# A transformer block on one core: token loads moved ahead of the weights, and side projections as whole-array matmuls

## The chip, the core and the metric

The kernel runs on one core of a Trainium2 chip. The core has a matrix engine (TensorE, PE in the profile, with its weight loads shown apart as PEld), a vector engine (VectorE, DVE), a scalar engine (ScalarE, ACT), a general engine (GpSimd, POOL) and a queue for transfers (SyncE, SP). The metric is the device time of one execution in microseconds.

## The reference

One block with two parallel branches on the same normalized input, 2048 tokens of width 512, 32 heads of 16:

```python
x = A_x                                   # [1, 2048, 512] bf16
xn = (x - mean) / sqrt(var + 1e-5)        # over the last axis
q, k, v = split(xn @ wqkv)                # 32 heads, 16 wide
p = softmax(q @ k.T / 4)                  # 2048 x 2048 for each head
attn = (p @ v) @ wo
h = silu(xn @ w1) * (xn @ w3)             # 512 -> 1792
return x + attn + h @ w2
```

## The kernel before

**The order is written by a planner.** A Python loop in `_build` keeps a clock for each engine, asks each engine's picker (`pick_pe`, `pick_act`, `pick_dve`, `pick_pool`, `pick_sp`) for its next candidate, emits the earliest, and notes what it reads and writes. The result is a fixed instruction stream for each engine, with semaphore waits between them. So a constant such as `TOL` or `A_LEAD` changes nothing in an instruction, but it changes where instructions stand.

**Attention.** The work is cut into units of one group of four heads and 256 queries (128 at the start and the end). It is done in two passes over the scores.

- Pass 1 (`p1_cand`, matmuls at L1011): score pairs, [128 queries x 512 keys] for two heads side by side, written to PSUM banks 0 and 1 or 2 and 3 in turn. VectorE takes the maximum over the keys (TENSOR_REDUCE at L1051, 1024 columns at a time, 1018 of them; three more pairs go through a custom instruction at L1040). A pair's banks are free again once its maximum is taken, so at most two pairs stand ahead of VectorE.
- The negated maximum of each query is then put into two spare rows of the queries (`tile_QT2`, the tiles named AQ, near the start and the end; a transpose by DMA for the rest), so that pass 2 produces scores with the maximum already subtracted.
- Pass 2 (`p2_cand`, matmuls at L1273): scores transposed, [128 keys x queries], 512 columns to a block, 2048 blocks, in banks 4 to 7. ScalarE takes the exponential (L1286, one block; L1316, two blocks in one instruction where two neighbours are ready) and writes PT.
- PT times the values with a column of ones (`tile_PV`) gives numerator and denominator.

Score matmuls contract over 32 rows only, so they use a quarter of the array's rows each, and up to four run at once ("row" mode of the planner).

**Side tiles.** Everything else on TensorE is a side tile: projections to keys, queries and values, gate and up projections, the output product (`tile_OUT`, `tile_OUTA`, `tile_OUTB`), and filler matmuls (`fill_cand`, `warm_cand` at L1626) whose result nobody reads, which are emitted when little else ran lately. All but the transposes (L645) and the warm-up go through one helper, `col_groups` (L552): a group is four matmuls of [128 rows x 32 columns], one for each column quarter of the array, that stream the same 512 columns side by side. `pick_pe` places a group, or its half of 256 columns, ahead of a waiting score matmul when it ends before that one is due:

```python
if c[0] + c[2] <= late + TOL:
    return c[0], c[1]
...
if len(c) > 3:
    if c[0] + _c_mm(256) <= late + TOL:
        return c[0], c[3]
```

The planner charges 0.106 us for a change from column groups to score rows and 0.092 us for the change back (`pe_start`).

**The head.** `LOADS = (0, "k", "q", 4, 8, 12)`: four token tiles of 128 tokens, key weights, query weights, then the other tokens, and value weights behind them, 512 KB each, all issued on SP in this order. VectorE takes each tile's statistics (L583, L586), GpSimd the inverse deviation (L596, L599), VectorE (L612) or GpSimd (L622) normalizes, as `NORM` says for each group of two tiles; TensorE transposes (L645) and ScalarE copies the transposed tile out (L652). ScalarE also pads the key and query weights (L523, L525) and takes the statistics of tiles 8 to 15 (L573, L577). When four tiles are there, `tile_KT(0)` projects their 512 keys in four groups of 512 columns, and `tile_QT` their 512 queries; ScalarE copies both out (L668, L764), and pass 1 can begin.

**The tail.** After the last maximum come the last unit's AQ tile and its copy (L782), its exponentials, its value product, a reciprocal (L1371), a product (L1373), the last output group, and the store.

Of the kernel before, what the change touches and what calls it, by code (L numbers as in the profile page):

```python
# [36 lines left out]
class _Prog:  # L37
# [3 lines left out]
    def __init__(self):  # L41
        self.ops = {e: [] for e in _ENGS}
        self.reg = {}
        self.ndma = 0
        self.dma_last = [None] * _NDMA_SEMS
        self.dma_final = [0] * _NDMA_SEMS
        self.free = {e: 0.85 for e in _ENGS}
        self.rg = [0.0] * 4
        self.pe_mode = "col"
        self.pe_vis = 0.0  # L50
        self.act_end = 0.0
# [83 lines left out]
    def pe(self, fn, reads, writes, mode, groups, dur, name="", first=None):  # L135
# [8 lines left out]
        start = self.pe_start(mode, groups, ready)  # L144
        if start < _COLD:
# [101 lines left out]
def _build(nc, A_x, A_wqkv, A_wo, B_w1, B_w3, B_w2, out):  # L247
# [15 lines left out]
    TOL = 0.02  # L263
    PV_LEFT = 4
    ROW_LEAD = 0.45
    PAIR_WAIT = 0.0
# [32 lines left out]
    FFN_HI = 600  # L299
# [11 lines left out]
    RECENT_MIN = 9400.0  # L311
# [27 lines left out]
    with ctx:  # L339
# [133 lines left out]
        NORM = "ddddpppp"  # L473
# [72 lines left out]
        def col_groups(bk, make_lhsT, rhs_ap, ncols, c0=0, start=True, stop=True, m=32, skip=False, n=4):  # L546
            def part(a, b, start, skip):
                def f(e):
                    for i in range(n):
                        kw = dict(skip_group_check=True) if skip else {}  # L550
# [4 lines left out]
                    return ins  # L555
                return f
# [7 lines left out]
        def ln_chunk(gi):  # L564
# [16 lines left out]
            else:  # L581
# [3 lines left out]
                for t in tl:  # L585
                    dveq.append(_Item(lambda e, t=t: e.bn_aggr(mv[:, t, :], stats[:, t, :]), [("st", t)], [("mv", t)],  # L586
                                      0.075, 0.2, pred=lambda t=t: ("st", t) in done, cb=lambda op: mv_done(op)))
# [39 lines left out]
        def tr_ready(t):  # L627
# [3 lines left out]
            if t % XG == XG - 1:  # L631
                gi = t // XG
                head_tiles.append(tile_KT(gi))
                if gi == 0:
                    head_tiles.append(tile_QT())

        def tile_tr(t):
# [11 lines left out]
            def evac(bk):  # L649
# [6 lines left out]
                         pred=lambda: ("xn", t) in done and (t < 4 or "QTg" in done))  # L656


        def tile_KT(sc):
            groups = []  # L660
            for c in range(DC):
                groups.append((lambda bk, c=c: col_groups(
                    bk, lambda i: wpad["k", 0][:, c, 32 * i:32 * i + 32],
# [3 lines left out]
            def evac(bk):  # L667
# [4 lines left out]
            return _Tile("KT0_%d" % sc, groups, evac,  # L672
                         pred=lambda: "wk0" in done
                         and all(("xnT", t) in done for t in range(sc * 4, sc * 4 + 4)))
# [3 lines left out]
        def tile_heads(what, g0, ng, sc, need):  # L678
# [4 lines left out]
            def grp(c):  # L683
                return lambda bk: col_groups(bk, lambda i: w[:, c, 64 * g0 + 32 * i:64 * g0 + 32 * i + 32],
# [45 lines left out]
        def tile_V(t, need=None):  # L730
            groups = []
            for c in range(DC):
                groups.append((lambda bk, c=c: col_groups(
                    bk, lambda i: xnT[:, c, t * 128 + 32 * i:t * 128 + 32 * i + 32], lambda i: wv[:, c, :], D,
# [12 lines left out]
        def qt_groups(qc, g, q0, nq, stop_last):  # L747
            groups = []
            for c in range(DC):
                groups.append((lambda bk, c=c: col_groups(  # L750
                    bk, lambda i: wpad["q", g][:, c, 32 * i:32 * i + 32],
# [5 lines left out]
        def qt0_done(op):  # L757
            done.add(("QT", 0))
            miscq.extend(act_stats[PRE_STATS:])

        def tile_QT():
            def evac(bk):
                done.add("QTg")
                return [_Item(lambda e: e.activation(QT[:, 0, :], bank(bk), ACTF.Identity),  # L764
                              [("ps", bk)], qh_keys(0, 0, 512), _c_act(512),
                              cb=qt0_done)]
            return _Tile("QT0", qt_groups(0, 0, 0, 512, True), evac,
                         pred=lambda: "wq0" in done and all(("xnT", t) in done for t in range(4)))

        def tile_QT2(u):  # L770
# [4 lines left out]
            for qt in range(nq // 128):  # L775
                groups.append((lambda bk, qt=qt: col_groups(
                    bk, lambda i: Z[:, par, qt, 32 * i:32 * i + 32], lambda i: ident[:, :], 128, c0=qt * 128,
# [18 lines left out]
        def ffn_pair(sc, fc):  # L796
# [18 lines left out]
            def groups(which):  # L815
                return [(lambda bk, c=c: col_groups(
                    bk, lambda i: w13[:, sl, which * DC + c, 32 * i:32 * i + 32],
# [3 lines left out]
            def zg_done(op):  # L821
                lazyq.append(_Item(lambda e: e.activation(th[:, ss, :], zg[:, ss, :], ACTF.Tanh),  # L822
                                   [("zg", ss)], [("th", ss)], _c_act(512), cb=part_done))
# [1082 lines left out]
```

## Time and profile before

| | us |
|---|---|
| runs shown (3) | 1202.22, 1201.60, 1201.04; median 1201.60 |
| profiled execution, its own time | 1200.68 |
| its span, first to last instruction | 1199.0 |
| VectorE busy | 1174.9 |
| ScalarE busy | 1167.5 |
| TensorE busy | 1152.8 |
| GpSimd busy | 453.6 |
| granted TensorE clock, mean | 0.999 of full speed |

The profiled execution's span is what all timeline positions count from; its own time is 1.68 us longer, and the median of the runs shown is 0.92 us above that. Busy time is the sum of the records of an engine where they do not overlap; a record includes the time from its start to the landing of its last result, so that two records that follow each other closely overlap, and a mean duration is longer than the beat at which such instructions follow each other. A bracket behind a timeline row gives the idle time ahead of it and what ended that.

### The profile page before, as it was taken

What the parts mean: (1) busy time and instruction counts of PE and PEld (TensorE: products, weight loads), DVE (VectorE), ACT (ScalarE), POOL (GpSimd) and SP (SyncE); (2) the same over time, 40 slices, a digit from 0 to 9 for tenths busy, and PEclk for the clock granted to TensorE, in tenths of its full rate; (3) what the DMA queues carried; (4) which work ended last, traced back from release to release, by engine and by line L of the source; (5) the groups of instructions that cost most, each with busy time, mean ns of one, the idle gap of its engine ahead of it and who ended that gap; (6) DMA issues with size and microseconds to landing.
All of it is one profiled execution on the core that took longest, in us unless ns stands there. A gap on an engine that the chain in (4) does not pass through costs nothing.

```text
span 1199.0 us, 44560 instructions
## 1 busy us (share of the span) xinstructions
PE 1152.8 (96%) x19488; PEld 476.3 (40%) x19488; DVE 1174.9 (98%) x1069; ACT 1167.5 (97%) x2210; POOL 453.6 (38%) x908
## 2 busy tenths in 40 slices
PE   9999999999999999999999999999999999999997
PEld 4443333343334433333334333333333343345554
DVE  8999999999999999999999999999999999999994
ACT  7799999999999999999999999999999999999997
POOL 4345655642212257442222236652222126233320
PEclk9999999999999999999999999999999999999999
DMA  6423214230001132210001122210000111001000
GB/s 194 117 51 91 64 40 112 44 71 25 20 19 33 31 70 50 53 33 21 22 16 27 33 59 48 62 42 20 23 20 20 36 47 25 19 22 22 23 12 25
DMA packets 131231, 52.86 MB, mean 44 GB/s; under 512 B 100068, under 2 KB 131036, under 8 KB 131036
## 3 DMA queue, kind: packets, MB, share of 16 engines
q1 hardware_dynamic: 131036, 50.01, 16.8%
q8 instruction: 153, 2.51, 0.9%
q14 instruction: 42, 0.34, 0.1%
HBM read 38.73 MB, written 6.74 MB: 38 GB/s over the span
## 4 chain that ended last, share of the span: by engine, by line
PE 47%; ACT 42%; DVE 9%; issue 1%; DMA 1%; POOL 1%; SPq 0%
ACT PT L1286 28%; PE ps L552 26%; PE ps L1273 13%; ACT PT L1316 9%; DVE part L1051 8%; PE ps L1011 7%; ACT zg L828 1%; ACT th L822 1%; ACT U L1381 1%; ACT ub L832 1%; ACT kq L723 1%; PE ps L645 0%; DMA PT<-in_A_x_dram 0%; DMA R<-rd 0%; POOL hT L811 0%
## 5 line engine op out<-in xcount | busy, mean ns | idle before, releaser
L1051 DVE TENSOR_REDUCE part<-ps 128x2 f32<-128x1024 f32 x1018 | 1154.8, 1212 | 1.5 <-PE ps L1011 0.5
L1286 ACT ACTIVATE PT<-ps 128x512 bf16<-128x512 f32 x1630 | 864.7, 631 | 9.5 <-PE ps L1273 4.9
L1273 PE MATMUL ps<-QT,KT 32*128 32x256 bf16 (+1 forms) x4672 | 536.0, 259 | 6.2 <-ACT PT L1316 5.6
L1011 PE MATMUL ps<-KT,QT 32*128 32x512 bf16 x2042 | 421.3, 384 | 1.6 <-DVE part L1051 1.5
L1273 PEld LDWEIGHTS ps<-QT,KT 32*128 32x128 bf16 x4672 | 203.1, 92 | 225.7 <-issue 89.9
L1316 ACT ACTIVATE PT<-ps 128x1024 bf16<-128x1024 f32 x209 | 221.6, 1081 | 0.0
L552 PE MATMUL ps<-xnT,ident 128*32 128x512 bf16 (+1 forms) x2620 | 198.1, 353 | 19.0 <-ACT PT L1316 9.8
L1406 POOL TENSOR_TENSOR Rc<-Lc,mone 128x8 f32<-128x8 f32 (+1 forms) x70 | 105.9, 1513 | 224.1 <-DMA Lc<-U 224.0
L552 PE MATMUL ps<-PT,Vaug 128*17 128x256 bf16 (+1 forms) x4672 | 179.8, 261 | 3.2 <-ACT PT L1316 2.1
L552 PE MATMUL ps<-xnT,w 128*32 128x512 bf16 (+1 forms) x2204 | 153.1, 345 | 6.5 <-ACT PT L1316 2.5
L1011 PEld LDWEIGHTS ps<-KT,QT 32*128 32x128 bf16 x2042 | 106.5, 91 | 131.7 <-issue 67.3
L552 PEld LDWEIGHTS ps<-PT,Vaug 128*17 128x17 bf16 x4672 | 87.1, 90 | 82.7 <-issue 60.7
L552 PEld LDWEIGHTS ps<-xnT,ident 128*32 128x32 bf16 x2620 | 54.3, 94 | 105.5 <-ACT PT L1286 46.7
L1158 POOL TENSOR_TENSOR mx<-part 128x16 f32<-128x16 f32 (+1 forms) x67 | 14.1, 210 | 174.4 <-DVE part L1051 174.4
L552 PEld LDWEIGHTS ps<-xnT,w 128*32 128x32 bf16 x2204 | 44.0, 95 | 81.6 <-issue 44.5
L552 PE MATMUL ps<-w,hT 128*32 128x256 bf16 (+1 forms) x1160 | 76.0, 336 | 0.0
L1426 POOL TENSOR_TENSOR wk_on<-U,R 128x256 bf16<-128x256 f32 (+1 forms) x37 | 23.4, 632 | 128.9 <-DMA R<-rd 128.9
L811 POOL TENSOR_TENSOR hT<-a,t 128x512 bf16<-128x512 f32 x56 | 71.2, 1271 | 2.3
L809 POOL TENSOR_TENSOR a<-zg,ub 128x512 f32<-128x512 bf16 x56 | 64.6, 1153 | 7.9 <-ACT ub L832 7.4
L1426 POOL TENSOR_TENSOR on_b<-U,R 128x256 bf16<-128x256 f32 (+1 forms) x33 | 23.5, 711 | 96.8 <-DMA R<-rd 96.6
L807 POOL TENSOR_SCALAR t<-th 128x512 f32<-128x512 bf16 x56 | 34.6, 619 | 27.6 <-ACT th L822 26.6
L822 ACT ACTIVATE th<-zg 128x512 bf16<-128x512 bf16 x56 | 39.2, 700 | 0.0
(98 smaller groups left out, 543.3 us busy)
## 6 DMA issues: line engine op xcount, KB each, us to landing
w<-in_B_w_dram SPq DMA_DIRECT2D x112, 128.0 KB
R<-rd SPq DMA_DIRECT2D x55, 128.0 KB
QT<-qd SPq DMA_DIRECT2D x31, 128.0 KB
KT<-kd SPq DMA_DIRECT2D x28, 128.0 KB
PT<-in_A_x_dram SPq DMA_DIRECT2D x4, 512.0 KB
xr<-in_A_x_dram SPq DMA_DIRECT2D x16, 128.0 KB
out_dram<-osb SPq DMA_DIRECT2D x16, 128.0 KB
qd<-kq SPq DMA_DIRECT2D x15, 128.0 KB
```

The source lines that it names most:

```text
L552: ins = e.matmul(bank(bk)[32 * i:32 * i + m, c0 + a:c0 + b], make_lhsT(i), rhs if (a, b) == (0, ncols) else rhs[:, a:b], start=start, stop ...
L807: q.append(_Item(lambda e: e.tensor_scalar(t1[:, :], th[:, ss, :], 1.0, 1.0, ALU.mult, ALU.add), [("th", ss)], [("t1",)], 0.62, 0.72))
L809: q.append(_Item(lambda e: e.tensor_tensor(a32[:, :], zg[:, ss, :], ub[:, ss, :], ALU.mult), [("zg", ss), ("ub", ss)], [("a32",)], 1.1, 1.25))
L811: q.append(_Item(lambda e: e.tensor_tensor(hT[:, hslot(idx), :], a32[:, :], t1[:, :], ALU.mult), [("a32",), ("t1",)], [("hT", hslot(idx))] ...
L822: lazyq.append(_Item(lambda e: e.activation(th[:, ss, :], zg[:, ss, :], ACTF.Tanh), [("zg", ss)], [("th", ss)], _c_act(512), cb=part_done))
L1011: ins = e.matmul(bank(2 * sl + i), QT[32 * j:32 * j + 32, qs, q * 128:(q + 1) * 128], KT[32 * j:32 * j + 32, g, c_ * 512:(c_ + 1) * 512], ...
L1051: redq.append(_Item(lambda e: e.tensor_reduce(dst, pair_ap.rearrange("p (a b) -> p a b", b=512), AX.X, ALU.max), writes, [("part", par, qt ...
L1273: ins = e.matmul(bank(b)[:, i * nq:(i + 1) * nq], KT[32 * j:32 * j + 32, g, (k0 + i) * 128:(k0 + i + 1) * 128], QT[32 * j:32 * j + 32, qs, ...
L1286: expq.append(_Item(lambda e: e.activation(PT[:, sl, :], bank(b), ACTF.Exp, scale=SCALE), [("ps", b)], [("PT", sl)], _c_act(512), cb=cb, e ...
L1316: return _Item(lambda e: e.activation(PT[:, s0:s1 + 1:s1 - s0, :], ps8[:, b0:b1 + 1:b1 - b0, :], ACTF.Exp, scale=SCALE), [("ps", b0), ("ps ...
L1406: poolq["nrm"].append(_Item(lambda e: e.tensor_tensor(Rc[:, pp, 0:nl], Lc[:, pp, 0:nl], mone[:, 0:nl], ALU.pow), [("Lc", pp), ("mone",)], ...
L1426: poolq["nrm"].append(_Item(lambda e: e.tensor_tensor(onorm[ob][:, g, q0:q0 + nq], U[:, us, 0:nq], R[:, pp, 0:nq], ALU.mult), [("U", us)] ...
```

## The change

Head:
- eight token tiles are loaded first, then key and query weights, then the rest;
- the keys of the first 512 tokens are projected tile by tile (four groups of 128 columns for each of four tiles, in one bank), each as soon as its tile is transposed, and still copied out at once;
- of the first 512 queries, 128 are projected and copied first (`QTa`), the other 384 behind them (`QTb`); units other than the first wait for `QTb`;
- the normalization of tiles 6 and 7 moves from VectorE to GpSimd (`NORM`).

Side tiles: where a group uses all four column quarters with 32 columns each, `col_groups` emits one matmul over the whole array, [128 rows x 128 columns], in place of four. Value products keep the four column quarters (17 columns each), and so do fillers right behind them. A group of 512 columns can be cut into pieces of 128, 256 or 384 (before: 256); `pick_pe` takes the largest piece that ends in time. The planner charges 0.095 us for a change between whole array and column quarters. Ten of its constants get other values.

```diff
@@ _Prog.pe
+        if mode == "col" and self.pe_mode == "col":
+            full = getattr(fn, "full", True)
+            if full != self.pe_full:
+                start = max(start, max(self.rg) + 0.095)
+        if mode == "col":
+            self.pe_full = getattr(fn, "full", True)
@@ constants
-    TOL = 0.02
-    PV_LEFT = 4
-    ROW_LEAD = 0.45
-    PAIR_WAIT = 0.0
+    TOL = 0.002
+    PV_LEFT = 5
+    ROW_LEAD = 0.46
+    PAIR_WAIT = 0.02
-    LAZY_MAX = 2.0
+    MIN_PIECE = 1
+    HI_LEAD = 0.0
+    LAZY_MAX = 3.0
-    LOADS = (0, "k", "q", 4, 8, 12)
+    LOADS = (0, 4, "k", "q", 8, 12)
-    A_LEAD = 0.7
-    RELAX = 0.0
+    A_LEAD = 0.69
+    RELAX = 0.03
-    FFN_HI = 600
+    FFN_HI = 800
-    RECENT_MIN = 9400.0
+    RECENT_MIN = 9800.0
-        NORM = "ddddpppp"
+        NORM = "dddppppp"
@@ col_groups
+            full = n == 4 and m == 32 and not own
...
+                    if full:
+                        return e.matmul(bank(bk)[:, c0 + a:c0 + b], make_lhsT(0, 128), rhs_ap(0)[:, a:b],
+                                        start=start, stop=stop, **kw)
                     for i in range(n):
...
             if ncols == 512:
-                f.halves = part(0, 256, start, True), part(256, 512, False, True)
+                f.piece = lambda a, b: part(a, b, start and a == 0, True)
+                f.at = 0
@@ tr_ready
-            if t % XG == XG - 1:
-                gi = t // XG
-                head_tiles.append(tile_KT(gi))
-                if gi == 0:
-                    head_tiles.append(tile_QT())
+            if t == 0:
+                head_tiles.append(tile_QT(0, 128, "QTa"))
+                head_tiles.append(tile_KT(0))
+            elif t == XG - 1:
+                head_tiles.append(tile_QT(128, 384, "QTb"))
+            elif t % XG == XG - 1:
+                head_tiles.append(tile_KT(t // XG))
@@ tile_KT
+            if sc == 0:
+                for t in range(XG):
+                    for c in range(DC):
+                        groups.append((lambda bk, c=c, t=t: col_groups(
+                            bk, lambda i, z=32: wpad["k", 0][:, c, 32 * i:32 * i + z],
+                            lambda i: xnT[:, c, t * 128:(t + 1) * 128], 128, c0=t * 128,
+                            start=(t, c) == (0, 0), stop=c == DC - 1, skip=True),
+                            [("wk0",)] + ON0_KEYS + [("xnT", t)], _c_mm(128), lambda t=t: ("xnT", t) in done))
@@ p1_cand
-                    if ("KT", 0, kc) in done:
+                    if ("KT", 0, kc) in done and (u == 0 or "QTb" in done):
@@ fill_cand
+            def emit_part(k):
+                P.pe(col_groups(bk, lambda i, z=32: ident[:, 32 * i:32 * i + z], lambda i: xnT[:, 0, 0:128 * k], 128 * k,
+                                own=P.pe_mode == "col" and not P.pe_full),
+                     [("ident",)] + xnT_keys(0, 128 * k), writes, "col", None, _c_mm(128 * k), name="fill")
@@ pick_pe
+            def fits(x, limit):
+                if len(x) < 4:
+                    return 9 if x[0] + x[2] <= limit else 0
+                return max([k for k in range(MIN_PIECE, x[4] + 1) if x[0] + _c_mm(128 * k) <= limit], default=0)
...
-            if c[0] + c[2] <= late + TOL:
-                return c[0], c[1]
-            if recent_cols(c[0]) < RECENT_MIN and c[0] <= end + URG_WAIT:
-                return c[0], c[3] if len(c) > 3 else c[1]
-            if len(c) > 3:
-                if c[0] + _c_mm(256) <= late + TOL:
-                    return c[0], c[3]
+            k = fits(c, late + TOL)
+            if not k and recent_cols(c[0]) < RECENT_MIN and c[0] <= end + URG_WAIT:
+                k = min(2, c[4]) if len(c) > 3 else 9
+            if k:
+                return c[0], (c[1] if len(c) < 4 or k >= c[4] else lambda: c[3](k))
             return go(x)
```

More of the change, by code (lines that the diff above doesn't have):

```diff
@@ L555, in f @@
                     return ins
+                f.full = full
                 return f
@@ L671, in evac @@
                               cb=lambda op: done.add(("KT", 0, sc)), name="first")]
-            return _Tile("KT0_%d" % sc, groups, evac,
+            return _Tile("KT0_%d" % sc, groups, evac, cols=2048 if sc else 512,
                          pred=lambda: "wk0" in done
-                         and all(("xnT", t) in done for t in range(sc * 4, sc * 4 + 4)))
+                         and all(("xnT", t) in done for t in range(sc * 4, sc * 4 + (4 if sc else 1))))
         kq_free = list(range(NKQ))
@@ L755, in qt_groups, with tile_QT, cb @@
             return groups
[L757 to L761, printed above, removed]
+        def tile_QT(q0, nq, name):
             def evac(bk):
[L763 to L768, printed above, removed]
+                def cb(op):
+                    done.add(name)
+                    if name == "QTa":
+                        done.add(("QT", 0))
+                    else:
+                        miscq.extend(act_stats[PRE_STATS:])
+                return [_Item(lambda e: e.activation(QT[:, 0, q0:q0 + nq], bank(bk)[:, 0:nq], ACTF.Identity),
+                              [("ps", bk)], qh_keys(0, q0, nq), _c_act(nq), cb=cb)]
+            return _Tile(name, qt_groups(0, 0, q0, nq, True), evac, cols=4 * nq,
+                         pred=lambda: "wq0" in done and all(("xnT", t) in done
+                                                            for t in range(q0 // 128, (q0 + nq) // 128)))
         def tile_QT2(u):
@@ L993, in p1_cand @@
             if ("QT", ug) not in done or any(("KT", g, c_) not in done for _, c_ in cells):
+                return None
+            if u and "QTb" not in done:
                 return None
@@ L1347, in f @@
                         return f2(e)
+                    f.full = False
                     return f
```

80 lines of the change are left out of this document (41 added, 39 removed).

## The prediction

> **What bounds the kernel now.** I read the page first (busy shares, then the groups), then the timeline of VectorE alone, then the head and the tail engine by engine, last TensorE's waits.
>
> ```profile
> span 1199.0 us, 44560 instructions
> ...
> PE 1152.8 (96%) x19488; PEld 476.3 (40%) x19488; DVE 1174.9 (98%) x1069; ACT 1167.5 (97%) x2210; POOL 453.6 (38%) x908
> ...
> L1051 DVE TENSOR_REDUCE part<-ps 128x2 f32<-128x1024 f32 x1018 | 1154.8, 1212 | 1.5 <-PE ps L1011 0.5
> L1286 ACT ACTIVATE PT<-ps 128x512 bf16<-128x512 f32 x1630 | 864.7, 631 | 9.5 <-PE ps L1273 4.9
> ```
>
> Three engines look full, so the shares do not tell which of them is the bound. VectorE's timeline does:
>
> ```profile
> 14.03 0.74 DVE L612 TENSOR_SCALAR osb<-PT,mv,lnr 128x512 bf16<-128x512 bf16 x2 [0.32 <-POOL lnr L599]
> 14.68 2.35 DVE L1051 TENSOR_REDUCE part<-ps 128x2 f32<-128x1024 f32 x2
> 17.54 26.76 DVE L1051 TENSOR_REDUCE part<-ps 128x2 f32<-128x1024 f32 x23 [0.51 <-PE ps L1011]
> ...
> 47.00 154.22 DVE L1051 TENSOR_REDUCE part<-ps 128x2 f32<-128x1024 f32 x136
> ...
> 1166.66 7.99 DVE L1051 TENSOR_REDUCE part<-ps 128x2 f32<-128x1024 f32 x7
> ```
>
> The row at 47.00 gives the beat: (154.22 - 1.21)/135 = 1.133 us from one maximum to the next. 1018 of these are 1153.4 us; three custom ones (1.21 + 0.08 less overlap, some 3.5) and six small maxima (0.09 net each) make 1157.4. The stream runs from 14.68 to 1174.65, 1160.0. So only 2.6 us between first and last maximum are not beat, and 0.51 of them are the one stall at 17.03. The middle can give at most some 2 us; what is left is the start (14.68) and the tail (1199.0 - 1174.65 = 24.35). ScalarE looks as full but is not: between 60 and 1150 us the start times of its single exponentials are never nearer than 0.476 us and 0.506 in the mean, so 1539 x 0.03 = 46 us of its "busy" time is waiting inside the record.
>
> **Part 1, the head.** What lies before 14.68, on ScalarE:
>
> ```profile
> 6.53 0.42 ACT L523 ACTIVATE wk_on<-wk_on 128x256 bf16<-128x256 bf16 x1 [3.86 <-DMA wk_on<-in_A_wqkv_dram]
> 8.04 0.42 ACT L525 ACTIVATE wk_on<-wq 128x256 bf16<-128x256 bf16 x1 [1.09 <-DMA wq<-in_A_wqkv_dram]
> ...
> 12.54 0.67 ACT L668 ACTIVATE KT<-ps,kbias 128x512 bf16<-128x512 f32 x1
> 13.29 0.60 ACT L764 ACTIVATE QT<-ps 128x512 bf16<-128x512 f32 x1
> ```
>
> The loads land 1.51 us apart (6.53 to 8.04). With eight token tiles first, tiles 4 to 7 land at 6.5, key weights at 8.04, query weights at 9.55, tiles 8 to 11 at 11.06. I follow the changed kernel's own order of instructions, with durations of before:
> - VectorE: statistics of tile 4 and one aggregate now stand ahead of the first normalization: 8.28 instead of 8.15; tiles 2 and 3 at 9.60 instead of 9.21 (their aggregate comes 0.66 later; from aggregate to normalization 1.27 as before).
> - ScalarE: transposed tiles 0 and 1 copied at 9.2 and 9.7; query weights padded at 10.15 (landed at 9.55, no wait); tiles 2 and 3 at 10.5 and 11.0; then one statistics pass (its cadence 0.76) at 11.5, before two; then the copy of 128 queries (0.16 cadence, the row of L782), then keys at 12.4.
> - TensorE: keys per token tile leave only tile 3's four matmuls (4 x 0.057, the spacing of the transposes) after the last copy, against 0.86 for four full groups before. They end behind the statistics pass, so they cost nothing; without that cover they would end at 12.2, still before 12.4.
> - Keys end at 13.1; the score pair starts at 13.15 and its maximum 0.41 to 0.43 later (the shortest distance in the trace): 13.6. VectorE is free by 12.4, since all its statistics and normalizations now stand ahead and tiles 6 and 7 went to GpSimd (+2 x 0.77 us there, in a queue whose keys are due only some 20 us in).
>
> In the head of before the query copy (13.29 to 13.89) and the normalizations at 14.03 ended last; both leave the path. Gain **1.1 us**. The other 384 queries are copied around 14.8 to 15.3; the third maximum needs them, and at 15.3 + 0.1 + 0.43 they come just before the second maximum ends (15.9), so the stall of 0.51 goes too, with some 0.1 us to spare. Bounds for the head: gain 0.6 (that margin missed, copies as late as before) to 1.8.
>
> **Part 2, whole-array side groups.** Four matmuls of 32 columns become one of 128: 19488 instructions fall to 14172, the streamed columns stay (side tiles 539392 in both; fillers 299008 to 301824). Is a whole-array group as fast, and is changing to it as cheap? Both stand side by side here:
>
> ```profile
> 26.11 0.39 PE L1011 MATMUL ps<-KT,QT 32*128 32x512 bf16 x2
> 26.43 0.40 PE L645 MATMUL ps<-ident,osb 128*128 128x128 bf16 x4
> 26.76 0.40 PE L552 MATMUL ps<-hT,xnT 128*32 128x512 bf16 x4
> 27.09 0.40 PE L645 MATMUL ps<-ident,osb 128*128 128x128 bf16 x4
> 27.42 0.39 PE L1011 MATMUL ps<-KT,QT 32*128 32x512 bf16 x2
> 27.74 0.62 PE L552 MATMUL ps<-hT,xnT 128*32 128x512 bf16 x8
> ```
>
> 512 columns are 0.213 us and four transposes 0.228; what remains of each 0.32 or 0.33 is 0.10 to 0.11 for a change of tiling, whichever way. Over all records a change from score rows to column tiles takes 0.090, to the whole array 0.107 (7 cases). In the two programs' orders the changes number 2508 and 2539: some 890 entries move from column tiles to the whole array (+0.017 each, 15 us), and 35 changes between whole array and value tiles are new (0.1 each, 3.5 us). That is 19 us of TensorE, beside other work: from the start times between 60 and 1150 us, TensorE neither streams nor changes over for 64 us. On the path: 0, between -1.5 and +3 for score pairs that come 17 ns later. (A pair's distance to its maximum is 0.41 at the least and 0.66 in the median, so few are that tight.) Against it, side pieces of 128 columns instead of 256 let a pair wait less.
>
> The Trainium skill, "TensorE: Matmul & The Clock Gate", section LDWEIGHTS, says a weight load takes its columns divided by 1.2, in ns: 107 for 128 columns. By that, 507 pieces of 128 columns would cost an estimated 25 us more of TensorE than their streaming. The trace differs: four transposes, each with its own 128-column load, run at a spacing of 57 ns.
>
> **Part 3, the retuned order.** ScalarE gets 1680 single exponentials and 184 pairs instead of 1630 and 209: 50 x 0.51 - 25 x 0.90 = +3.0 us, inside its 46 us of waiting. At the last score pair TensorE has issued 2012 of 2048 blocks instead of 2015, and behind the last query copy ScalarE has 27 singles and 2 pairs instead of 24 and 3: 3 x 0.51 - 0.90 = +0.6 us in the tail, which is all exponentials:
>
> ```profile
> 1176.36 0.28 ACT L782 ACTIVATE QT<-ps 128x128 bf16<-128x128 f32 x1
> 1176.76 1.58 ACT L1286 ACTIVATE PT<-ps 128x512 bf16<-128x512 f32 x3
> 1178.78 2.80 ACT L1286 ACTIVATE PT<-ps 128x512 bf16<-128x512 f32 x5 [0.44 <-PE ps L1273]
> 1182.46 0.60 ACT L1286 ACTIVATE PT<-ps 128x512 bf16<-128x512 f32 x1 [0.89 <-PE ps L1273]
> ```
>
> One exponential more ahead of that copy costs 0.3 net of an idle 0.25. The gap of 0.89 comes from an output group that waits for a reciprocal; in the new order that value tile is finished one batch earlier, which I credit with 0.4. Tail: **+0.5**, from -2 (all gaps gone) to +1.5.
>
> **Sum.** -1.1 - 0.5 + 0.0 + 0.5 = -1.1 us. The profiled execution took 1200.68 (1.68 around its span); the median of the runs shown is 0.92 higher. So 1199.6 profiled, 1200.5 as a median. A difference under 0.2% (2.4 us) is about what a measurement of this kernel can tell from none.
>
> **Rivals.**
> - *Late score pairs* (slower). Each entry to the whole array is 17 ns longer than the planner's constant; every pair behind one comes later. It decides once pairs slip by over 0.15 us, where about a quarter of the distances (those under 0.56) touch the floor: 250 x 0.02 to 0.05 us is 5 to 12 us, 1206 to 1213. For: 5% of the distances already are under 0.44. Against: finer pieces, and TensorE idles again every few us. Chance 0.18.
> - *TensorE becomes the bound* (slower). If a 128-column load (0.097 us in the transposes' rows) cannot hide at each of 890 entries, 86 us go against 64 of slack: +20 or more, 1220 to 1240. The same would follow if a whole-array stream counted less with the clock (now 0.999). Against: 57 ns per transpose, 0.107 per entry, and the warm-up here was whole-array matmuls alone. Chance 0.06.
> - *The middle and the tail close up* (faster). Finer pieces remove the 2 us that are not beat, and the tail loses its gaps (0.25 + 0.44 + 0.89): a further 3 us, 1197.5. For: at 17.03 and at 1181.6 a side group stands in front of the row group that is late. Chance 0.24.
> - *The change gains nothing*, because ScalarE's first exponential (46.77) does not come earlier and its backlog of three blocks, 1.5 us, is paid in the tail: 1201.6, inside "same". Chance 0.12.
>
> **Chances.** The forecast itself has 0.40, with 1199.3 to 1202.0 as its own range. Faster by over 0.2% (under 1199.2): most of the third rival and the forecast's edge, 0.28. Slower (over 1204.0): the first two, 0.24. Within: 0.48. The range takes in the third rival and the near end of the first: 1197.0 to 1206.0.
>
> **What would show it.** Right: first maximum at 13.6, no stall before the third, stream 1159 to 1160 long, 24.5 to 25.3 behind it, whole-array groups of 512 at 0.216 spacing. Wrong: a first maximum at 14.3 or later; maxima waiting for L1041 over 5 us in total; entries to whole-array groups longer than 0.12; a granted clock under 0.99.

## The result

| | before | after |
|---|---|---|
| median of 6 runs each, us | 1201.42 | 1196.31 |
| lowest and highest | 1200.67 to 1202.22 | 1195.78 to 1196.78 |
| profiled execution, its own time | 1200.68 | 1196.41 |
| its span | 1199.0 | 1194.7 |
| granted TensorE clock | 0.999 | 0.999 |

The ratio is 0.9957 (95% interval 0.9944 to 0.9970): faster by 0.43%. The forecast of 1200.5 is 4.2 us too high, and the measured time lies 0.7 us under the low end of its range.

From the page of the changed kernel, the lines that answer to those shown of before:

```profile
span 1194.7 us, 33930 instructions
...
PE 1154.4 (97%) x14172; PEld 482.5 (40%) x14172; DVE 1172.0 (98%) x1067; ACT 1169.5 (98%) x2236; POOL 455.3 (38%) x912
...
L1081 DVE TENSOR_REDUCE part<-ps 128x2 f32<-128x1024 f32 x1018 | 1153.0, 1217 | 1.9 <-PE ps L1041 1.7
L1316 ACT ACTIVATE PT<-ps 128x512 bf16<-128x512 f32 x1680 | 889.2, 628 | 5.6 <-PE ps L1303 2.5
```

TensorE has 5316 matmuls fewer and is as busy as before (1154.4 against 1152.8), so a count of instructions tells nothing here. VectorE's maxima still are the bound. Its idle time before the maxima even rose in the page, from 1.5 to 1.9 us; 1.44 of that is the wait for the very first one, and most of the rest is one row. VectorE's timeline shows it:

```profile
13.60 27.30 DVE L1081 TENSOR_REDUCE part<-ps 128x2 f32<-128x1024 f32 x24 [1.44 <-PE ps L1041]
41.15 2.36 DVE L1081 TENSOR_REDUCE part<-ps 128x2 f32<-128x1024 f32 x2 [0.24 <-PE ps L1041]
...
46.10 678.01 DVE L1081 TENSOR_REDUCE part<-ps 128x2 f32<-128x1024 f32 x599
...
1162.48 8.02 DVE L1081 TENSOR_REDUCE part<-ps 128x2 f32<-128x1024 f32 x7
```

The first maximum starts at 13.60. The stall before the third is gone: the first row now runs through 24 maxima. From 46.10 on, 599 maxima follow without a bracket. The mean distance in that row is (678.01 - 1.22)/598 = 1.1318 us; in before's row of 136 it was (154.22 - 1.21)/135 = 1.1334. Behind that is no change of the beat, but late maxima that no bracket shows: between 60 and 1150 us nine of ten distances are 1.130 to 1.132 us in both kernels, and the distances over 1.16 us number 19 in before and 6 in after; they are 2.09 and 0.61 us longer in sum than that many at 1.1315. The last maximum ends at 1170.50 (1174.65 before).

To place the difference I add up, for all maxima, the distance to the next one less the beat of 1.1315 us (less 0.075 for each small maximum in between, and less 1.2065 for each custom one). What is left is the time by which maxima came late. "Head" is the sum up to 60 us, "middle" from 60 to 1150 us. "Left" counts the blocks of 512 columns that ScalarE still has to exponentiate when the last maximum ends, and "tail" is the time from there to the end of the span (the last maximum counted as 1.21 us long in every kernel).

| kernel | median us | ratio to before (95%) | span | first max. | head | middle | tail | left |
|---|---|---|---|---|---|---|---|---|
| before | 1201.42 | | 1199.0 | 14.68 | 1.62 | 2.42 | 24.29 | 32 |
| after | 1196.31 | 0.9957 (0.9944, 0.9970) | 1194.7 | 13.60 | 0.65 | 0.29 | 24.21 | 34 |
| e1_quarters | 1199.03 | 0.9987 (0.9978, 0.9996) | 1196.8 | 13.70 | 1.72 | 1.34 | 24.14 | 34 |
| e2_whole | 1201.87 | 1.0008 (0.9999, 1.0017) | 1199.6 | 14.43 | 0.53 | 4.96 | 23.55 | 32 |
| e3_head | 1203.84 | 1.0023 (1.0013, 1.0033) | 1201.8 | 13.98 | 1.72 | 4.53 | 25.58 | 36 |
| e4_side | 1199.75 | 0.9986 (0.9977, 0.9995) | 1198.5 | 14.65 | 0.59 | 1.61 | 25.68 | 36 |
| e5_oldconst | 1201.59 | 1.0007 (0.9999, 1.0016) | 1201.8 | 14.29 | 1.17 | 1.83 | 28.52 | 42 |
| e6_newconst_on_before | 1206.79 | 1.0041 (1.0029, 1.0053) | 1205.6 | 14.62 | 1.93 | 2.13 | 30.94 | 42 |
| e7_oldtanh | 1199.17 | 0.9985 (0.9974, 0.9996) | 1197.2 | 13.56 | 0.66 | 1.11 | 25.89 | 38 |
| e8_halves | 1223.68 | 1.0184 (1.0167, 1.0200) | 1224.7 | 13.27 | 0.60 | 17.97 | 36.94 | 56 |
| e9_whole_in_head | 1200.17 | 0.9991 (0.9982, 1.0000) | 1198.3 | 14.59 | 0.51 | 2.49 | 24.77 | 32 |
| e10_quarters_in_head | 1197.87 | 0.9970 (0.9959, 0.9982) | 1196.5 | 14.65 | 1.64 | 0.32 | 23.95 | 34 |
| e11_control | 1199.34 | 0.9985 (0.9976, 0.9993) | 1197.3 | 13.46 | 0.66 | 0.94 | 26.25 | 38 |
| e12_measured_changes | 1203.56 | 1.0021 (1.0012, 1.0030) | 1201.5 | 13.21 | 0.54 | 2.01 | 29.74 | 44 |

Every ratio is against runs of the kernel before on the same chip (their medians there were 1200.99 to 1201.42). The kernel after was timed beside the first of these alone, so a difference from its median can hold some 0.4 us that belong to the chip. The other columns are of the one profiled execution of each kernel; for e5_oldconst and e8_halves that was a long one, 1.9 and 2.8 us over the median. From before to after the span falls by 4.27 us: 1.08 at the first maximum, 0.97 in the head, 2.13 in the middle, 0.08 in the tail.

The change also raises the planner's charge for ScalarE's tanh (L851) from 0.477 to 0.52 us, a line that the diff above leaves out; e7_oldtanh is about it.

### The profile page after: what moved, and what is told of

It reads as the page before. It is cut to its first block, busy times and chain, and to the rows that moved or that the text cites. A ratio compares the mean times of both kernels' runs of the same rounds, so it can differ in the third digit from the quotient of the medians.

```text
span 1194.7 us, 33930 instructions
## 1 busy us (share of the span) xinstructions
PE 1154.4 (97%) x14172; PEld 482.5 (40%) x14172; DVE 1172.0 (98%) x1067; ACT 1169.5 (98%) x2236; POOL 455.3 (38%) x912
## 4 chain that ended last, share of the span: by engine, by line
PE 45%; ACT 44%; DVE 6%; issue 2%; DMA 2%; POOL 1%; ACTq 0%; POOLq 0%
ACT PT L1316 30%; PE ps L562 17%; PE ps L1303 13%; PE ps L566 8%; ACT PT L1346 7%; PE ps L1041 7%; DVE part L1081 6%; ACT zg L856 2%; ACT th L850 1%; ACT ub L860 1%; DMA R<-rd 1%; ACT U L1412 1%; ACT kq L750 1%; PE ps L1663 1%; DMA Lc<-U 0%
## 5 line engine op out<-in xcount | busy, mean ns | idle before, releaser
L1316 ACT ACTIVATE PT<-ps 128x512 bf16<-128x512 f32 x1680 | 889.2, 628 | 5.6 <-PE ps L1303 2.5
L1303 PE MATMUL ps<-QT,KT 32*128 32x256 bf16 (+1 forms) x4672 | 544.5, 259 | 4.7 <-ACT PT L1346 3.7
L1303 PEld LDWEIGHTS ps<-QT,KT 32*128 32x128 bf16 x4672 | 207.4, 92 | 214.1 <-issue 110.7
L1346 ACT ACTIVATE PT<-ps 128x1024 bf16<-128x1024 f32 x184 | 194.6, 1075 | 0.0
L562 PE MATMUL ps<-xnT,ident 128*128 128x512 bf16 (+3 forms) x646 | 177.4, 341 | 17.5 <-DVE part L1081 6.7
L562 PE MATMUL ps<-xnT,w 128*128 128x512 bf16 (+3 forms) x637 | 153.2, 321 | 4.7 <-ACT ub L860 1.3
L562 PEld LDWEIGHTS ps<-xnT,ident 128*128 128x128 bf16 x646 | 47.4, 97 | 99.9 <-ACT PT L1316 44.5
L562 PEld LDWEIGHTS ps<-xnT,w 128*128 128x128 bf16 x637 | 44.9, 97 | 85.6 <-issue 52.9
L562 PE MATMUL ps<-w,hT 128*128 128x512 bf16 (+3 forms) x330 | 75.1, 315 | 0.0
```

The lines of the kernel that those rows point to most:

```text
L562: return e.matmul(bank(bk)[:, c0 + a:c0 + b], make_lhsT(0, 128), rhs_ap(0)[:, a:b], start=start, stop=stop, **kw)
L1303: ins = e.matmul(bank(b)[:, i * nq:(i + 1) * nq], KT[32 * j:32 * j + 32, g, (k0 + i) * 128:(k0 + i + 1) * 128], QT[32 * j:32 * j + 32, qs, ...
L1316: expq.append(_Item(lambda e: e.activation(PT[:, sl, :], bank(b), ACTF.Exp, scale=SCALE), [("ps", b)], [("PT", sl)], _c_act(512), cb=cb, e ...
L1346: return _Item(lambda e: e.activation(PT[:, s0:s1 + 1:s1 - s0, :], ps8[:, b0:b1 + 1:b1 - b0, :], ACTF.Exp, scale=SCALE), [("ps", b0), ("ps ...
```

## The experiments

Three causes were to be told apart: the head's new load and key order; the form of the side groups (one whole-array matmul or four quarters) with no instruction moved; and the new order in the middle that the smaller pieces and the constants give. The granted clock of the profiled executions was 0.997 or more in the mean, and 0.982 in e8_halves. A mean can hide a short fall: besides e8_halves, the clock fell to half for 3.4 us in e4_side (from 805.6) and in e5_oldconst (from 742.2), and maxima came late there:

```profile
805.00:809.00 4.00, 3.48 (x23) 1.05 (x20) 3.61 (x4) 3.15 (x6) 2.79 (x2) 0.57 0.04 5
742.00:746.00 4.00, 3.78 (x46) 1.48 (x50) 3.33 (x3) 3.65 (x7) 2.89 (x8) 0.57 0.12 33
```

The first row is of e4_side, the second of e5_oldconst. Such a row gives a stretch and its length, then the busy time and number of instructions of PE, PEld, DVE, ACT and POOL, then the granted clock, the DMA share and GB/s.

**e1_quarters: after's order, four quarters again.**

```diff
-                    if full:
-                        return e.matmul(bank(bk)[:, c0 + a:c0 + b], make_lhsT(0, 128), rhs_ap(0)[:, a:b],
-                                        start=start, stop=stop, **kw)
```

> The changed kernel with its order of instructions kept, but every whole-array matmul of the side tiles emitted as four matmuls of 32 columns again. Theory 'order' (the gain of the middle comes from where the smaller pieces stand, not from the form of the matmul): 1196 to 1198, first maximum still at 13.6, maxima that wait for a score pair about as few as in the changed kernel. Rival 'whole array' (leaving the whole array for score rows takes 0.098 us where leaving four quarters takes 0.107, and there are a quarter of the instructions): the 880 exits cost 8 us of TensorE time more, score pairs slip, and 2 us or more of the gain go: 1198.5 to 1201.

The span is 2.15 us longer than after's: 1.07 in the head, 1.05 in the middle, 0.10 at the first maximum, and -0.07 in the tail. The medians are 2.7 us apart. So with after's order the whole array is worth 2 us or a little more, as the rival had it, and about half of it falls in the first 47 us. TensorE's timeline there, after first and then e1_quarters, from the same score pair to the next one:

```profile
16.37 0.39 PE L1041 MATMUL ps<-KT,QT 32*128 32x512 bf16 x2
16.69 0.34 PE L562 MATMUL ps<-xnT,wk_on 128*128 128x384 bf16 x1
16.86 0.61 PE L664 MATMUL ps<-ident,osb 128*128 128x128 bf16 x8
17.31 0.22 PE L562 MATMUL ps<-hT,xnT 128*128 128x128 bf16 x1
17.46 0.39 PE L1041 MATMUL ps<-KT,QT 32*128 32x512 bf16 x2
```

```profile
16.66 0.39 PE L1038 MATMUL ps<-KT,QT 32*128 32x512 bf16 x2
16.98 0.35 PE L563 MATMUL ps<-xnT,wk_on 128*32 128x384 bf16 x4
17.26 0.62 PE L661 MATMUL ps<-ident,osb 128*128 128x128 bf16 x8
17.81 0.24 PE L563 MATMUL ps<-hT,xnT 128*32 128x128 bf16 x4
17.98 0.39 PE L1038 MATMUL ps<-KT,QT 32*128 32x512 bf16 x2
```

The work is the same, and the next pair comes 1.09 us later in the one and 1.32 in the other. The eight transposes are whole-array matmuls (128\*128). With quarter groups around them TensorE changes its tiling on the way in and on the way out, 17.26 - 16.98 = 0.28 against 16.86 - 16.69 = 0.17, and again behind them, 0.55 against 0.45. 1.32 is longer than VectorE's beat of 1.13: the maximum of the second pair starts 0.17 us late in e1_quarters, at 18.41, 0.42 behind its matmuls, and in after on the beat. Between 13.6 and 60 us quarter and whole-array groups follow each other directly 12 times in before, 13 in e1_quarters, 12 in e3_head and 16 in e10_quarters_in_head, with head sums of 1.62, 1.72, 1.72 and 1.64; and once in after, never in e2_whole and e9_whole_in_head, twice in e4_side, with 0.65, 0.53, 0.51 and 0.59.

**e2_whole: before's order, whole-array groups.**

```diff
+            full = n == 4 and m == 32 and not own
...
+                    if full:
+                        return e.matmul(bank(bk)[:, c0 + a:c0 + b], make_lhsT(0, 128), rhs_ap(0)[:, a:b],
+                                        start=start, stop=stop, **kw)
```

> The kernel before with its order kept, but the four matmuls of each side group emitted as one over the whole array; head, pieces and constants as before. 'Order': 1200.5 to 1201.5, no different from before within 1 us. 'Whole array': the stream of maxima loses its 2 us of stalls in the middle, 1198.5 to 1199.8. My own prediction of 17 ns more at each entry would show as 1201.5 to 1204.

The same edit on the other order does not help: 1201.87, no measurable difference. (That lies in the range given for a longer entry; but the entry was not 17 ns longer, see below.) The head gains its 1.09 us here too. But the middle loses 2.54. This order was laid out where a side group and a value product shared a tiling. With whole-array groups there are now 77 direct changes between the two in the middle (38 in after, whose planner charges for them). Since the two kernels have the same instructions in the same order, each maximum can be compared with its twin: 1.2 to 1.5 of the 2.54 us (by whether the distance ahead of a maximum or behind it is taken) fall on the 173 maxima that have such a change close by (up to 1.5 us before their start or while they run), the rest is spread thin. That the changes cause this half is likely by where it falls, but not shown; the other half stays open.

**e9_whole_in_head and e10_quarters_in_head: the form in the head alone, no instruction moved.** The first is before with whole-array groups up to the 28th pair, the second is after with quarters up to there.

```diff
+            full = n == 4 and m == 32 and not own and p1_n[0] < 28
```

> The kernel before with its order kept, whole-array matmuls only in groups emitted before the 28th score pair (some 45 us), four quarters afterwards. Theory 'mixed tilings' (in the head the transposes take the whole array and the side groups its quarters; a dozen changes between the two at 0.1 us each stall the maxima there): stalls before 60 us 1.1 us less, the middle as before, 1199.8 to 1200.5. If whole-array groups do not matter there: 1201 to 1201.5.

```diff
+            whole = full and p1_n[0] >= 28
...
-                    if full:
+                    if whole:
```

> The changed kernel with its order kept, four quarters in place of the whole array only in groups planned before the 28th score pair. 'Mixed tilings': stalls before 60 us 1.1 us more than in the changed kernel, the middle as there: 1197.2 to 1197.8. If the whole array matters only through its cheaper exits (0.098 for 0.107 us) in the middle: 1196.2 to 1196.8.

VectorE's timeline, e9_whole_in_head and then e10_quarters_in_head:

```profile
14.60 28.54 DVE L1056 TENSOR_REDUCE part<-ps 128x2 f32<-128x1024 f32 x25
```

```profile
14.65 28.11 DVE L1082 TENSOR_REDUCE part<-ps 128x2 f32<-128x1024 f32 x24 [2.11 <-PE ps L1042]
```

25 maxima in 28.54 us are a beat of 1.139, 24 in 28.11 one of 1.170; neither row has a bracket inside, and the second lost 0.7 us all the same. The head sums move by -1.11 and +0.99, the middles by under 0.1. In the times: 0.9991 (0.9982, 1.0000) for the first, a bare gain; 1197.87 against after's 1196.31 for the second. So the 1 us in the head comes from the form of the side groups beside the transposes. In e9_whole_in_head queries and keys are copied as in before, at one go, and the stall before the third maximum is gone nevertheless.

e10_quarters_in_head also has after's load order and begins at 14.65, because in that execution the transposed tiles were copied at 10.0 and not at 9.4. The first of them was normalized by 8.83, but on TensorE the warm-up matmuls stand ahead of the transposes, in after and then in e10_quarters_in_head:

```profile
2.40 6.71 PE L1663 MATMUL ps<-ones_t 128*128 128x256 bf16 x39
```

```profile
2.40 7.36 PE L1664 MATMUL ps<-ones_t 128*128 128x256 bf16 x39
```

In every kernel these start 0.213 us apart at first and 0.109 later. The step from one to the other comes at 7.06 us in after, at 8.51 here, at 8.35 in e5_oldconst and at 5.4 to 6.9 in the others. Where it came by 6.4, the transposes begin 0.44 to 0.47 us behind the start of the first normalization, that is, right behind its end; in after they begin 0.87 behind its start, here 1.15, and in e5_oldconst 1.36. So one profile does not fix the start. Of the nine kernels with the new load order the first maximum is at 13.60 in the median (13.21 to 14.65), of the five with the old at 14.62 (14.43 to 14.68).

**e3_head and e4_side: each half alone.** e3_head is before with the load order, the keys by tile, the 128 queries first and `NORM`; e4_side is after without them.

```diff
-    LOADS = (0, "k", "q", 4, 8, 12)
+    LOADS = (0, 4, "k", "q", 8, 12)
...
-        NORM = "ddddpppp"
+        NORM = "dddppppp"
```

> The kernel before with the head's part of the change alone (loads, keys by token tile, 128 queries first, tiles 6 and 7 normalized on GpSimd); side groups, pieces and constants as before. 'Head': first maximum at 13.6 instead of 14.68 and no stall of 0.51 at 17.03, 1199.3 to 1200.3. If the head brings all of it (the later stream differing by chance of the order): 1196 to 1197.5. If ScalarE paces the kernel and an earlier start is given back later: 1201 to 1202.

> The changed kernel with the old head (loads, keys in four groups of 512 columns, 512 queries at once, tiles 6 and 7 normalized on VectorE). 'Order' and 'whole array' both: first maximum back at 14.7, the middle as short as in the changed kernel: 1197.5 to 1199.5. If the head brings all: 1200.5 to 1202.

e3_head starts 0.70 earlier and ends 2.9 later. The planner, given another start, writes another order; the middle loses 2.11 and the tail 1.29 (36 blocks left). Its head stays at 1.72: copying 128 queries first does not help it while the side groups are quarters. e4_side gains 0.81 in the middle and 1.03 in the head and gives back 1.39 in the tail (36 left). In its middle, 0.94 us came late in three maxima from 808.5 to 811.2, at the fall of its clock; that is most of the 1.3 us by which its middle is behind after's. The spans of the two halves, +2.9 and -0.5, do not add up to the -4.3 of both. What one part does to the order is larger than what it does by itself.

**e5_oldconst, e6_newconst_on_before, e7_oldtanh: the constants.** After with the nine old values, before with the nine new ones and the new charge for the tanh, after with the old charge alone.

```diff
-    TOL = 0.002
-    PV_LEFT = 5
+    TOL = 0.02
+    PV_LEFT = 4
...
-    RECENT_MIN = 9800.0
+    RECENT_MIN = 9400.0
```

> The changed kernel with nine of its constants at the values of before (TOL, PV_LEFT, ROW_LEAD, PAIR_WAIT, LAZY_MAX, A_LEAD, RELAX, FFN_HI, RECENT_MIN). Theory 'constants' (the retuned planner constants shorten the middle): stalls of the maxima between 60 and 1150 us back to those of before or more, +2 us or more, 1198 to 1201. Theory 'pieces' (pieces of 128 and 384 columns do it): 1196 to 1197.5.

> The kernel before with the nine new constants and the planner's new cost for the tanh (0.52 for 0.477 us); head, groups and pieces as before. 'Constants': the middle loses about 2 us, 1199 to 1200. 'Pieces': 1201 to 1203, no gain, since whole or half groups cannot use the smaller tolerance.

```diff
-                                   [("zg", ss)], [("th", ss)], 0.52, cb=part_done))
+                                   [("zg", ss)], [("th", ss)], _c_act(512), cb=part_done))
```

> The changed kernel with the planner's old cost for the tanh of the gate (0.477 us, where the trace has 0.519 from start to start, 56 times). If that correction matters, every plan behind a tanh is 0.042 us early on ScalarE and score blocks wait: 1197.5 to 1199. If not (the waits on ScalarE resynchronize the engines): 1196 to 1197.

With the old values after loses its gain (1201.59). In the profiled execution that is 1.54 in the middle, 4.31 in the tail, and 1.21 up to 60 us, of which 0.69 is a later first maximum, behind the late warm-up; and 0.88 of the 1.54 came late in two maxima at 744.3 and 746.0, at the fall of its clock. What is left of the middle is no more than the control below shows; what remains is the tail. On before the new ones gain 0.29 in the middle and lose 6.7 in the tail. Both end with 42 blocks left. So the new values are not good in themselves. The run with the old charge for the tanh is 0.8 longer in the middle and 1.7 in the tail by the profile, 2.9 in the median; after the control below, that need not be the charge.

**e8_halves: the new tolerance without the new pieces**, groups of 512 columns cut at 256 only.

```diff
-                return max([k for k in range(MIN_PIECE, x[4] + 1) if x[0] + _c_mm(128 * k) <= limit], default=0)
+                return max([k for k in {2, x[4]} if x[0] + _c_mm(128 * k) <= limit], default=0)
```

> The changed kernel with pieces of 256 and 512 columns alone, as before; constants, head and whole-array groups kept. 'Pieces': more score pairs at the shortest distance to their maximum (about 5% instead of 1 to 2%), the stream 1.5 to 2.5 us longer, 1198 to 1199.5. 'Constants': 1196 to 1197.5.

1223.68, far worse than any estimate, and not by the pieces alone. Windows of the profile show where:

```profile
60.00:400.00 340.00, 320.98 (x3573) 129.30 (x3610) 339.13 (x301) 335.47 (x636) 142.63 (x259) 1.00 0.20 50
400.00:600.00 200.00, 190.97 (x1996) 72.38 (x2015) 193.09 (x171) 190.43 (x365) 82.92 (x144) 0.94 0.16 39
...
464.00:466.00 2.00, 2.00 (x22) 0.48 (x18) 1.70 (x2) 1.68 (x4) 0.00 (x0) 0.50 0.00 0
```

Up to 400 us the clock is full, and there the maxima are late by 1.33 us more than after's (1.26 against -0.07). For the other orders drawn from after (e7_oldtanh, e11_control, e12_measured_changes) that figure is 0.0 to 0.6 us, so a part of it is likely the pieces' doing, and no run shows how much. From 464 to 487 us, from 733 to 737 and from 843 to 856 the granted clock is 0.50, and the sums from 400 to 800 and from 800 to 1150 us are 9.7 and 6.7 us above after's. With that ScalarE falls behind, 56 blocks are left, and the tail is 36.94.

**e11_control and e12_measured_changes: how much is the draw of an order?** The first changes one constant of the planner by a thousandth; in a line by line comparison of the two traces some 1800 of TensorE's 14172 matmuls then stand elsewhere. The second puts the changes of tiling as measured (below) into the planner, which should only make its clock truer.

```diff
-    A_LEAD = 0.69
+    A_LEAD = 0.691
```

> The changed kernel with A_LEAD 0.691 for 0.690: no part of the change is undone, but about half of TensorE's order comes out otherwise. It measures what the order alone is worth without any reason behind it. If the planner's order is robust: 1196 to 1197. If the order is a lottery of a few us: anything from 1196 to 1200, with another number of blocks left behind the last maximum.

```diff
-            t = max(t, max(self.rg) + (0.092 if self.pe_mode == "row" else 0.0))
+            t = max(t, max(self.rg) + (0.093 if self.pe_mode == "row" else 0.0))
...
-                t = max(t, max(self.rg) + 0.106)
+                t = max(t, max(self.rg) + (0.098 if self.pe_full else 0.107))
```

> The changed kernel with the planner's costs of a change of tiling as the trace has them (into side groups 0.093 for 0.092, from whole array to score rows 0.098, from quarters to rows 0.107, for 0.106). If the middle is governed by how true these are: the stream 0.5 to 1.5 us shorter, 1194.5 to 1196. If the order is a lottery: 1196 to 1200.

The control costs 3.0 us in the median (1199.34), 2.0 of its span in the tail and 0.7 in the middle. The truer planner costs 7.2 (1203.56), 5.5 of it in the tail. A change without any meaning of its own thus moves this kernel by as much as the effects that are looked for. The tail reads the same way in every kernel. ScalarE's timeline after the last query copy, in after:

```profile
1172.38 0.28 ACT L810 ACTIVATE QT<-ps 128x128 bf16<-128x128 f32 x1
1173.08 1.57 ACT L1316 ACTIVATE PT<-ps 128x512 bf16<-128x512 f32 x3 [0.41 <-PE ps L1303]
1175.28 3.04 ACT L1316 ACTIVATE PT<-ps 128x512 bf16<-128x512 f32 x6 [0.63 <-PE ps L1303]
...
1181.16 8.05 ACT L1316 ACTIVATE PT<-ps 128x512 bf16<-128x512 f32 x16
```

Behind that copy the control has smaller gaps (0.20 and 0.31) and ends later, because 35 blocks are left there and not 31: four more at some 0.5 us. Over all fourteen kernels 32 to 34 blocks left go with a tail of 23.6 to 24.8 us, 36 to 38 with 25.6 to 26.3, 42 to 44 with 28.5 to 30.9, 56 with 36.9. After has one of the good draws.

Of the ranges given ahead, those of e1_quarters (the rival's), e9_whole_in_head and e11_control (a lottery) were met; e4_side, e5_oldconst, e7_oldtanh and e10_quarters_in_head came out 0.1 to 0.6 us above the one that fits best; e3_head, e6_newconst_on_before, e8_halves and e12_measured_changes lie above every range.

## Why the prediction was wrong

- **Part 1, the first maximum: right, with some luck.** 13.6 was predicted and 13.60 measured, and ScalarE's rows come as followed. They are, in after's timeline:

```profile
7.84 0.42 ACT L532 ACTIVATE wk_on<-wk_on 128x256 bf16<-128x256 bf16 x1 [5.17 <-DMA wk_on<-in_A_wqkv_dram]
9.37 1.08 ACT L671 ACTIVATE xnT<-ps 128x512 bf16<-128x512 bf16 x2 [1.11 <-PE ps L664]
10.34 0.42 ACT L534 ACTIVATE wk_on<-wq 128x256 bf16<-128x256 bf16 x1
10.68 1.08 ACT L671 ACTIVATE xnT<-ps 128x512 bf16<-128x512 bf16 x2
...
12.28 0.27 ACT L792 ACTIVATE QT<-ps 128x128 bf16<-128x128 f32 x1
12.43 0.69 ACT L695 ACTIVATE KT<-ps,kbias 128x512 bf16<-128x512 f32 x1
```

  Each is within 0.2 us of the step that named it (9.2, 10.15, 10.5, 12.4). But two misses cancel: the first normalization starts at 8.08, not 8.28, and the transposes then wait some 0.4 us for the warm-up matmuls, which the prediction left out. Where the warm-up ended early, a head of the same design starts at 13.21 (e12_measured_changes) and 13.27 (e8_halves), and the two heads with the same instructions, e1_quarters and e10_quarters_in_head, start at 13.70 and 14.65.
- **The stall of 0.51: its size half, its cause wrong.** The prediction gave it to the late copy of the queries. The runs give the head 1.0 us, and the two kernels that change only the form show it whole: direct changes between quarters and whole array beside the transposes, 12 before and 1 after. The prediction counted 35 *new* changes of that sort in the middle, where TensorE has slack, and missed the 11 removed in the one stretch where it has none. The timeline of before that it shows had one: transposes, quarter groups, transposes, each 0.32 or 0.33 apart.
- **Part 2, 0.0 for the form in the middle: this step failed.** The entry of 0.107 was taken from seven rows, and these were of transposes. In after, whole-array side groups start a median 0.093 behind a score row (transposes 0.104), quarters 0.091; and the way back, which the prediction did not price, is 0.098 from the whole array and 0.107 from quarters, counted from the first matmul of the group. The last of four quarter matmuls starts 0.010 behind the first, and counted from it the way back is 0.099 too: what the whole array saves is the start of three more matmuls. A visit is so some 7 ns cheaper and not 17 dearer. With after's order this form is worth 1.05 us in the middle.
- **The Trainium skill's rule** of 107 ns for a weight load of 128 columns ("TensorE: Matmul & The Clock Gate", section LDWEIGHTS) would have cost an estimated 25 us. No run shows that: in after, 96 of 100 whole-array matmuls that follow each other directly start their streaming time plus 1 to 15 ns apart, and pieces of 128 columns a median of 66 ns before the next. The same page's section "Wait — 56ns, not 53.3ns?" has 55.6 ns for 128 columns; the transposes agree with it (a median of 56), the pieces are 10 ns above.
- **Part 3, the middle's order at 0: wrong.** The other 1.1 us of the middle's 2.1 (before to e1_quarters) come from the order. How well pairs keep ahead can be seen in the distance from a pair's last matmul to its maximum, where 0.41 is the floor: one in twenty is under 433 ns in before, 456 in e1_quarters, 494 in e8_halves and 550 in after, and under 427 in e2_whole. So the new order alone raises it little, and the whole-array form more, where the order was laid out for it. That the smaller pieces do it is not shown. The third rival, *The middle and the tail close up*, had the size in the middle, 2 us, and put all of it down to the pieces; it was given 0.24.
- **The room in the stream: too small.** The prediction took a row's mean, 1.133, for the beat, and found 2.6 us between the first and last maximum that are not beat. With 1.1315, the distance that nine of ten keep, 4.0 us are not (1.62 and 2.42), and 3.1 of them went.
- **The tail, +0.5: measured -0.1.** The count was right (27 singles and 2 pairs behind the last copy). ScalarE's idle time behind that copy fell from 1.60 to 1.07 us, a little more than the 0.4 credited. The rest is mostly the beat: the last row of 16 exponentials has (8.05 - 0.60)/15 = 0.497 us each, and the sum had used 0.51.
- **The range.** The span's fall is 1.08 + 0.97 + 2.13 + 0.08, of which the prediction had 1.08 and half of the second. So 2.1 us in the middle and half a microsecond in the head were put at nothing, and the tail 0.6 too high: this is why the time fell under the range. The medians differ by 0.8 us more than the two profiled executions, since before's profiled one was a short one among its runs. The larger fault is that nothing was set aside for the planner's draw. One thousandth in one constant moves the median by 3.0 us, and a part of after's 5.1 us may be of that kind. How much is due to each constant can't be said from these runs, since any one of them redraws the order; that stays open. What is shown with the order held is 1.0 us (head) and 1.05 us (middle) for the form.
- **The slower rivals.** *Late score pairs* fell with the entry of 0.093. *TensorE becomes the bound* fell with the clock at 0.999 and the spacing above; e8_halves, some 20 us longer, shows that it was no empty fear, but there the clock decides. *The change gains nothing* was wrong: ScalarE's first exponential comes at 45.96 and not 46.77.

## What to carry to other kernels

Where a planner writes the order, test an edit with the order held fixed, by changing only what is emitted, and run one control with a meaningless change before giving a few microseconds to any constant. When the tiling of the matrix engine changes, count the direct changes that go away as well as those that come, and price them where that engine has no slack; an average over the span hides both. A timeline row without brackets can still hide a stall: look at the distances of its instructions one by one, since the mean of a row mixes the beat with the late ones. And look at the granted clock of each stretch, not at its mean, before a loss in one stretch is put down to the edit.

## What the runs showed of the hardware

- A change of tiling costs, beyond the streaming of the group before, a median of 91 ns from score rows to quarters, 93 to the whole array, 98 from the whole array to score rows, 107 from quarters to score rows, 96 from the whole array to quarters and 107 back. Both figures of 107 count from the first of four quarter matmuls; from the last, which starts 10 ns behind it, they are 99. The Trainium skill's page "TensorEngine Tiling (Array Packing)", section Key Properties, says that a change of mode drains TensorE; the trace has a gap at these changes, and these are its sizes here.
- The warm-up matmuls of 256 columns start 0.213 us apart from 2.4 us on, and 0.109 apart from a moment on that lies between 5.4 and 8.5 us in the fourteen executions. What stands behind them waits accordingly.
- In e8_halves the granted clock fell to 0.50 for some 23 us (464 to 487) while TensorE's records covered 9.53 of the 10 us from 460 to 470. In the timeline, the 5.5 us ahead of that hold only score rows of 32 rows and value products of 17 columns. Longer such stretches, up to 9.2 us at 537 us in the same kernel, did not lower it; and in e5_oldconst and e4_side it fell for 3.4 us with a whole-array side matmul 0.3 and 2.1 us before. So what set it off stays open. The page "TensorE: Matmul & The Clock Gate" of the Trainium skill, in its first part, ties the clock to how busy TensorE was of late; the busy share of the profile, at any rate, did not tell of the fall here.
